# Sixteen attention items in float32: the product with v taken with the queries on partitions, a column of sums in v, and the division moved behind the product

## The chip, the cores and the metric

The kernel runs on one core of one Trainium2 chip. The metric is the device time of one launch in microseconds, the median of several runs. Five engines work side by side on it: TensorE (PE, its weight loads are listed as PEld), VectorE (DVE), ScalarE (ACT), GpSimd (POOL) and SyncE (SP), which here issues every transfer between memory and the on-chip buffers.

## What is computed

Attention with a window of 128 keys, then two feed-forward layers over the 2304 resulting tokens. Batch 4, heads 8, sequence 576, head size 64; d_model 512, d_ff 2048.

```python
scores = scale * np.matmul(q, k.transpose(0, 1, 3, 2))
scores = np.where(mask, scores + bias[None], -1000000000.0)
scores = scores - np.max(scores, axis=-1, keepdims=True)
attn = np.exp(scores)
attn = attn / (np.sum(attn, axis=-1, keepdims=True) + 1e-09)
attn_out = np.matmul(attn, v)
x = attn_out.transpose(0, 2, 1, 3).reshape(B * S, H * D)
h = x @ w_in;  g = np.maximum(h, 0.0) + alpha * np.minimum(h, 0.0);  x = g @ w_out
h = x @ w_in2; g = h * (1.0 / (1.0 + np.exp(-1.702 * h)));  out = g @ w_out2
```

The weights arrive as 64-bit floats and are decoded on the chip.

## The kernel before, in words

**Attention.** The work is cut into 64 items `(b, u, h)`: a batch, one of two pieces of the sequence (u = 0: queries 0 to 255; u = 1: the other 320) and a head. Items 0 to 15 (b = 0 and 1 of u = 0; `n < FP`) multiply in plain float32, which PE runs as two passes for every matmul; their rows in the trace count both. All later items split each operand into two parts of a faster type and take other branches. The steps of an item: `a_qk` (scores `s`, line 343), `a_bias` (DVE adds the position bias and takes the row minimum, 363), `a_exp` (ACT, 379, which also sums each row), `a_recip` (DVE, 387 and 388), `a_norm` (the weights `tt` times the reciprocal: one chunk of 128 keys on DVE, 399, one of 256 on ACT, 397), `a_trans` (PE transposes `tt` into `pt`, 412), `a_pt_hi` (ACT copies `pt` to the on-chip buffer, 419), `a_av` (PE multiplies with v, 433), `a_x3` (ACT rounds the result `x` into `xh`, 480, and DVE puts the rest into `xl`, 107).

For items 0 to 15 two heads share one result: `vz` holds v in one half of its columns and zeros in the other, so an even head fills partitions 0 to 63 of `x` and the odd head partitions 64 to 127. So `a_x3` works once for a pair of items. The tiles `s`, `pt` and `x` come from one pool of four banks (`ps_a`).

**First layer.** Blocks k of 256 tokens; block k of u = 0 needs the eight items of batch k. For each of 16 slices f of d_ff: `m1_h` (12 products into `h`, line 494, reading `xh`, `xl` and the weights `wh`, `wl`), an activation (ACT 509, DVE 519, ACT 523 and DVE 107 into `gh`, `gl`), and `m1_o`, two slices later (12 products into `o`, 545). Block 0 needs all of items 0 to 7, block 1 all of items 8 to 15.

**Weights.** The first layer has 32 chunks of 512 KB. A chunk is loaded into one of four `ws` buffers (131), scaled by ACT (147, 148), joined by DVE (152 `sign`, 157 `shift`, 162 `add`), rounded by ACT into `wh` (102) and the rest put into `wl` by DVE (107). The load of chunk i + 4 waits for the `add` of chunk i.

**Order.** The program is written as a loop over items 0 to 9 (lines 734 to 765) with two decode steps an item, then as steps (k, f) with an item every two steps (781 to 846). A scheduler with a timeline of its own puts the instructions of each engine in a fixed order from that; each engine runs its own list in order and waits where an operand is missing.

Of the kernel before, what the change touches and what calls it, by code (L numbers as in the profile page):

```python
# [11 lines left out]
F32 = mybir.dt.float32  # L12
# [3 lines left out]
AF = mybir.ActivationFunctionType  # L16
ALU = mybir.AluOpType
PSUM = bass.MemoryType.PSUM

B, H, S, D = 4, 8, 576, 64  # L20
NT, DM, DFF = 2304, 512, 2048
P = 128
# [12 lines left out]
         chunks=((256, 128, 128, 256), (384, 128, 256, 256), (512, 64, 384, 192))),  # L35
# [12 lines left out]
FP = 2 * H  # L48
# [17 lines left out]
def tile_window_attention__then__two_mlps(  # L66
# [13 lines left out]
    nc = tc.nc  # L80
# [10 lines left out]
    ident = const.tile([P, P], F32, name="ident")  # L91
# [30 lines left out]
    chunks = [(0, f, part) for f in range(NF) for part in range(2)]  # L122
# [134 lines left out]
    ps_a = at.enter_context(tc.tile_pool(name="ps_a", bufs=4, space=PSUM))  # L257
# [3 lines left out]
    sts = [ap_.tile([P, 16], F32, name=f"st{i}") for i in range(2)]  # L261
# [3 lines left out]

    af = ExitStack()
    apf = af.enter_context(tc.tile_pool(name="attf", bufs=1))
    vzs = [apf.tile([P, 2, P], F32, name=f"vz{i}") for i in range(2)]
    pts = [apf.tile([P, 384], F32, name=f"pt{i}") for i in range(2)]
    relht = apf.tile([P, H, 2 * P], BF16, name="relht")  # L270

# [13 lines left out]
    st = {}  # L285

    def raw_of(n):
        return (raws + rawfs)[n % 4] if n < H else raws[n % 2]
# [34 lines left out]
    @stage  # L323
    def a_split_v(n, b, u, h, U):
        nv = (2, 4)[u]
        vr = raw_of(n)[:, UCOLS[u] - nv * D : UCOLS[u]].rearrange("p (j d) -> p j d", d=D)
        if n < FP:
            d0 = (h % 2) * D
            nc.gpsimd.tensor_copy(vzs[n % 2][:, :, d0 : d0 + D], vr)
            return  # L330
        vp = ar["v", n % 2]
        nc.scalar.copy(vp[:, :nv, :D], vr)
        sub("pool", vp[:, :nv, D:], vr, vp[:, :nv, :D])
# [40 lines left out]
    @stage  # L374
    def a_exp(n, b, u, h, U):
        tt, s = tts[n % 2], sts[n % 2]
        for i, (c0, rows, kk, keys) in enumerate(U["chunks"]):
            t = tt[:rows, i * 256 : i * 256 + keys]
            nc.scalar.activation(
                t, t, AF.Exp, bias=s[:rows, i : i + 1], scale=-1.0, accum_out=s[:rows, 4 + i : 5 + i]  # L380
            )

    @stage
    def a_recip(n, b, u, h, U):
        s = sts[n % 2]
        m = len(U["chunks"])
        nc.vector.tensor_scalar(s[:, 8 : 8 + m], s[:, 4 : 4 + m], 1e-9, None, op0=ALU.add)
        nc.vector.reciprocal(s[:, 12 : 12 + m], s[:, 8 : 8 + m])  # L388

    @stage  # L390
    def a_norm(n, b, u, h, U, eng):
        tt, s = tts[n % 2], sts[n % 2]
        for i, (c0, rows, kk, keys) in enumerate(U["chunks"]):
            t = tt[:rows, i * 256 : i * 256 + keys]
            r = s[:rows, 12 + i : 13 + i]
            if eng == "act" or (eng == "mix" and i):
                nc.scalar.mul(t, t, r)
            else:
                nc.vector.tensor_scalar(t, t, r, None, op0=ALU.mult)
# [27 lines left out]
    @stage  # L427
    def a_av(n, b, u, h, U):
        if n < FP:
            x = st["x", n] = st["x", n - 1] if h % 2 else ps_a.tile([P, 512], F32, tag="a", name="x")  # L430
            pt, vz = pts[n % 2], vzs[n % 2]
            for j in range(2):
                nc.tensor.matmul(  # L433
                    x[:, j * P : 256], vz[:, j, :], pt[:, j * 256 : 256 + j * P],
                    start=(h % 2 == 0 and j == 0), stop=(h % 2 == 1 and j == 1), skip_group_check=True,
                )
            return
        vp = ar["v", n % 2]
        x = ps_a.tile([P, 512], F32, tag="a", name="x")
        js = (0, 1) if u == 0 else (2, 1, 3, 4)  # L440
        for i, j in enumerate(js):
            col, nq, oc = PTCOL[u][j]
            v = vp[:, j - U["k0"] // P, :]
            for k, p in enumerate((ar["pth"], ar["ptl"])):
                nc.tensor.matmul(  # L445
                    x[:, oc : oc + nq], v, p[:, col : col + nq],
                    start=(i == 0 and k == 0), stop=(i == len(js) - 1 and k == 1),
                    skip_group_check=True,
                )
        st["x", n] = x  # L450
# [17 lines left out]
    @stage  # L468
    def a_x3(n, b, u, h, U):
        if h % 2 == 0:  # L470
            return
        nq, c, xp = U["nq"], h // 2, xps
        if n < FP:
            xp = st["x", n]
        t = u * B * UNITS[0]["nq"] + b * nq
        done = 0
        while done < nq:
            r = (t + done) % RING
            w = min(nq - done, RING - r)
            nc.scalar.copy(xh[:, c, r : r + w], xp[:, done : done + w])  # L480
            sub("dve", xl[:, c, r : r + w], xp[:, done : done + w], xh[:, c, r : r + w])
            done += w
# [222 lines left out]


    for t in vzs:
        nc.gpsimd.memset(t, 0.0)
    for t in sts:
        nc.gpsimd.memset(t, 1.0)  # L710
    def w_first(n):
# [54 lines left out]
    n = H + 2  # L766
# [14 lines left out]
    for s, (k, f) in enumerate(steps):  # L781
        n = H + 2 + s // 2
# [181 lines left out]
```

## Time and profile before

| | us |
|---|---|
| median of 3 runs | 968.03 (967.75 to 969.53) |
| the profiled execution | 967.92 |
| its span, first to last instruction | 966.1 |
| PE busy | 939.6 (97%) |
| DVE busy | 721.6 (75%) |
| ACT busy | 536.4 (56%) |
| POOL busy | 89.8 (9%) |

The page gives busy time for the whole span. The kernel has a first stage of some 60 us, in which weights are decoded and items 0 to 9 are worked on side by side, and a long rest in which PE hardly pauses, so the shares of the whole say little of the first stage. For it the views by stretch of time and the rows of each engine in order of time are read.

### The profile page before, as it was taken

The page shows a single profiled execution, that of the slowest core. Times are in us where ns is not written, and L with a number is a line of the kernel's source. Part 1 is how long each engine was busy: PE and PEld are TensorE (multiplying, and loading weights), DVE is VectorE, ACT ScalarE, POOL GpSimd, SP SyncE. Part 2 cuts the span into 40 slices and gives each one's busy share as a digit, 9 for nine tenths or more (in the row PEclk, how much of TensorE's full clock was granted, in tenths as well). Part 3 has the DMA queues.
Part 4 walks back from the last instruction along what each step waited for, and adds up shares of the span by engine and source line. Part 5 has one row for each costly group of instructions (what it writes and reads, how often), then busy time and mean ns, then how long its engine had stood idle before and what let it go on. Part 6 is the DMA issues. An engine that isn't in the chain of part 4 may idle for free.

```text
span 966.1 us, 17886 instructions
## 1 busy us (share of the span) xinstructions
PE 939.6 (97%) x6536; PEld 871.2 (90%) x6536; DVE 721.6 (75%) x1789; ACT 536.4 (56%) x1343; POOL 89.8 (9%) x127
## 2 busy tenths in 40 slices
PE   5899999999999999999999999999999999999997
PEld 3579889999999999999988888888898889999997
DVE  6998967767888888887666864697233798878876
ACT  6987766666767667676534443564232644333433
POOL 1000021122222222222000000000000000000000
PEclk9999999999999999999999999999999999999999
DMA  8654521222222223212022335566432333443323
GB/s 266 187 185 148 184 79 56 78 72 66 89 67 88 67 66 89 67 66 89 1 69 81 124 112 182 186 219 200 155 113 88 140 140 114 142 142 113 132 85 109
DMA packets 43895, 112.44 MB, mean 116 GB/s; under 512 B 5024, under 2 KB 15008, under 8 KB 43808
## 3 DMA queue, kind: packets, MB, share of 16 engines
q1 hardware_dynamic: 43808, 111.31, 35.3%
q8 instruction: 51, 0.84, 0.3%
q14 instruction: 36, 0.29, 0.1%
HBM read 82.98 MB, written 28.31 MB: 115 GB/s over the span
## 4 chain that ended last, share of the span: by engine, by line
PE 92%; DMA 3%; ACT 2%; DVE 1%; issue 1%; SPq 0%; DVEq 0%; ACTq 0%
PE h L494 21%; PE h L592 20%; PE p L659 17%; PE o L545 17%; PE p L545 5%; PE x L445 3%; PE pt L412 3%; DMA ws<-in_w_out_dram 2%; PE s L352 1%; PE s L353 1%; PE s L343 1%; PE x L433 1%; ACT ws L148 1%; DMA ws<-in_w_in_dram 0%; ACT oh L102 0%
## 5 line engine op out<-in xcount | busy, mean ns | idle before, releaser
L494 PE MATMUL h<-xh,wh 128*128 128x256 f32 (+1 forms) x512 | 153.7, 302 | 1.0 <-ACT xh L480 0.7
L494 PE MATMUL h<-xh,wl 128*128 128x256 f32 (+1 forms) x512 | 153.6, 300 | 0.0
L494 PE MATMUL h<-xl,wh 128*128 128x256 f32 (+1 forms) x512 | 153.5, 300 | 0.1
L659 PE MATMUL p<-wh,oh 128*128 128x256 f32 x504 | 136.2, 284 | 1.0 <-ACT oh L102 0.6
L659 PE MATMUL p<-wl,oh 128*128 128x256 f32 x504 | 136.1, 283 | 0.0
L545 PE MATMUL o<-gh,wl 128*128 128x256 f32 x448 | 127.5, 286 | 0.0
L545 PE MATMUL o<-gh,wh 128*128 128x256 f32 x448 | 125.4, 286 | 0.0
L545 PE MATMUL o<-gl,wh 128*128 128x256 f32 x448 | 125.2, 281 | 0.0
L659 PE MATMUL p<-wh,ol 128*128 128x256 f32 x504 | 119.2, 284 | 1.0 <-DVE ol L107 1.0
L592 PE MATMUL h<-x2h,wh 128*128 128x512 f32 (+1 forms) x320 | 117.8, 368 | 0.0
L592 PE MATMUL h<-x2l,wh 128*128 128x512 f32 (+1 forms) x320 | 117.7, 368 | 0.0
L592 PE MATMUL h<-x2h,wl 128*128 128x512 f32 (+1 forms) x320 | 117.7, 368 | 0.0
L606 DVE TENSOR_TENSOR g<-h,sg 128x512 f32<-128x512 f32 (+1 forms) x80 | 51.0, 637 | 79.6 <-ACT sg L602 79.5
L602 ACT ACTIVATE sg<-h 128x512 f32<-128x512 f32 (+1 forms) x80 | 44.5, 556 | 107.2 <-PE h L592 106.9
L494 PEld LDWEIGHTS h<-xh,wh 128*128 128x128 f32 x512 | 97.9, 192 | 6.7 <-ACT xh L480 1.9
L494 PEld LDWEIGHTS h<-xl,wh 128*128 128x128 f32 x512 | 98.5, 192 | 5.0 <-DVE st L388 1.3
L494 PEld LDWEIGHTS h<-xh,wl 128*128 128x128 f32 x512 | 98.3, 192 | 2.9
L659 PEld LDWEIGHTS p<-wh,oh 128*128 128x128 f32 x504 | 96.4, 192 | 2.1 <-ACT oh L102 2.0
L659 PEld LDWEIGHTS p<-wl,oh 128*128 128x128 f32 x504 | 96.7, 192 | 0.1
L519 DVE SCALAR_TENSOR_TENSOR g<-n,beta,h 128x256 f32<-128x256 f32 x112 | 53.2, 476 | 46.6 <-ACT n L509 46.4
L659 PEld LDWEIGHTS p<-wh,ol 128*128 128x128 f32 x504 | 86.3, 192 | 1.7 <-DVE ol L107 1.6
L509 ACT ACTIVATE n<-h 128x256 f32<-128x256 f32 x112 | 42.8, 384 | 79.9 <-PE h L494 79.5
(107 smaller groups left out, 2270.7 us busy)
## 6 DMA issues: line engine op xcount, KB each, us to landing
ws<-in_w_in_dram SPq DMA_DIRECT2D x32, 512.0 KB, 3.6
ws<-in_w_out_dram SPq DMA_DIRECT2D x32, 512.0 KB, 3.9
raw<-in_u_dram SPq DMA_DIRECT2D x32, 512.0 KB, 3.4
g2d<-g SPq DMA_DIRECT2D x32, 512.0 KB, 3.4
gr<-g2d SPq DMA_DIRECT2D x32, 512.0 KB, 3.2
raw<-in_u_dram SPq DMA_DIRECT2D x16, 320.0 KB, 2.8
wd<-x2d SPq DMA_DIRECT2D x36, 128.0 KB, 3.0
out_dram<-ob SPq DMA_DIRECT2D x16, 256.0 KB, 3.9
```

Of the source, the lines that this page charges most:

```text
L148: pin(nc.scalar.mul(lo, lo.bitcast(U32), 2.0**-29))
L343: nc.tensor.matmul(o[:, :keys], raw[:, c0 : c0 + rows], raw[:, 256 + kk : 256 + kk + keys], start=True, stop=True)
L412: nc.tensor.transpose(banks[bank][:, dst : dst + P], src, ident)
L445: nc.tensor.matmul(x[:, oc : oc + nq], v, p[:, col : col + nq], start=(i == 0 and k == 0), stop=(i == len(js) - 1 and k == 1), skip_group_ ...
L494: nc.tensor.matmul(ph, w[:, 0, c * P : (c + 1) * P], x[:, c, r : r + n], start=(c == 0 and i == 0), stop=(c == NC - 1 and i == 2),)
L509: nc.scalar.activation(n, ph, AF.Relu, scale=-1.0)
L519: nc.vector.scalar_tensor_tensor(g, n, beta[:, f : f + 1], ph, op0=ALU.mult, op1=ALU.add)
L545: nc.tensor.matmul(o, w[:, 1, c * P : (c + 1) * P], g, start=(f == 0 and (k == KM or c % 2 == 0) and i == 0), stop=(f == NF - 1 and i == 2 ...
L592: nc.tensor.matmul(ph[:, :n], w[:, f % 2, c * P : (c + 1) * P], x[:, c, :n], start=(c == 0 and i == 0), stop=(c == NC - 1 and i == 2),)
L602: nc.scalar.activation(sg[:, :n], ph[:, :n], AF.Sigmoid, scale=1.702)
L606: nc.vector.tensor_tensor(g[:, f % 2, :n], ph[:, :n], sg[:, :n], op=ALU.mult)
L659: nc.tensor.matmul(o[:, m, :], g[:, a, m * P : (m + 1) * P], w, start=(p == 0 and m == 0 and i == 0), stop=(p == NF // 2 - 1 and i == 2), ...
```

## The change

For items 0 to 15 the transposed weights `pt` become the stationary operand and v the moving one, so the result `xq` has the queries on partitions. `vz` has 65 columns a key block: 64 of v and one of ones, so the last column of `xq` is the sum of the (not yet divided) weights. There are three matmuls an item, of 65 columns each, in place of one of 256 and one of 128. `a_exp` no longer sums, `a_recip` and `a_norm` do nothing for these items. After the odd item of a pair DVE adds 1e-9 to the four sums of the pair, takes the reciprocals and multiplies `xq` by them into the buffer tile `xq` (lines 445, 446, 448 of the changed kernel). `a_x3` first transposes that back with two PE transposes a pair into a new tile `x` (line 488), and goes on as before.

```diff
--- before.py
+++ after.py
@@ -265,7 +265,8 @@
 
     af = ExitStack()
     apf = af.enter_context(tc.tile_pool(name="attf", bufs=1))
-    vzs = [apf.tile([P, 2, P], F32, name=f"vz{i}") for i in range(2)]
+    vzs = [apf.tile([P, 2, D + 1], F32, name=f"vz{i}") for i in range(2)]
+    xq = apf.tile([P, 2, 2, D], F32, name="xq")
     pts = [apf.tile([P, 384], F32, name=f"pt{i}") for i in range(2)]
     relht = apf.tile([P, H, 2 * P], BF16, name="relht")
 
@@ -325,8 +326,7 @@
         nv = (2, 4)[u]
         vr = raw_of(n)[:, UCOLS[u] - nv * D : UCOLS[u]].rearrange("p (j d) -> p j d", d=D)
         if n < FP:
-            d0 = (h % 2) * D
-            nc.gpsimd.tensor_copy(vzs[n % 2][:, :, d0 : d0 + D], vr)
+            nc.gpsimd.tensor_copy(vzs[n % 2][:, :, :D], vr)
             return
         vp = ar["v", n % 2]
         nc.scalar.copy(vp[:, :nv, :D], vr)
@@ -376,6 +376,9 @@
         tt, s = tts[n % 2], sts[n % 2]
         for i, (c0, rows, kk, keys) in enumerate(U["chunks"]):
             t = tt[:rows, i * 256 : i * 256 + keys]
+            if n < FP:
+                nc.scalar.activation(t, t, AF.Exp, bias=s[:rows, i : i + 1], scale=-1.0)
+                continue
             nc.scalar.activation(
                 t, t, AF.Exp, bias=s[:rows, i : i + 1], scale=-1.0, accum_out=s[:rows, 4 + i : 5 + i]
             )
@@ -384,13 +387,15 @@
     def a_recip(n, b, u, h, U):
         s = sts[n % 2]
         m = len(U["chunks"])
+        if n < FP:
+            return
         nc.vector.tensor_scalar(s[:, 8 : 8 + m], s[:, 4 : 4 + m], 1e-9, None, op0=ALU.add)
         nc.vector.reciprocal(s[:, 12 : 12 + m], s[:, 8 : 8 + m])
 
     @stage
     def a_norm(n, b, u, h, U, eng):
         tt, s = tts[n % 2], sts[n % 2]
-        for i, (c0, rows, kk, keys) in enumerate(U["chunks"]):
+        for i, (c0, rows, kk, keys) in enumerate(U["chunks"] if n >= FP else ()):
             t = tt[:rows, i * 256 : i * 256 + keys]
             r = s[:rows, 12 + i : 13 + i]
             if eng == "act" or (eng == "mix" and i):
@@ -427,13 +432,20 @@
     @stage
     def a_av(n, b, u, h, U):
         if n < FP:
-            x = st["x", n] = st["x", n - 1] if h % 2 else ps_a.tile([P, 512], F32, tag="a", name="x")
+            x = st["xq", n] = st["xq", n - 1] if h % 2 else ps_a.tile([P, 2, 2, D + 1], F32, tag="a", name="xq")
             pt, vz = pts[n % 2], vzs[n % 2]
-            for j in range(2):
+            for c, j, col in ((0, 0, 0), (1, 0, 128), (1, 1, 256)):
                 nc.tensor.matmul(
-                    x[:, j * P : 256], vz[:, j, :], pt[:, j * 256 : 256 + j * P],
-                    start=(h % 2 == 0 and j == 0), stop=(h % 2 == 1 and j == 1), skip_group_check=True,
+                    x[:, c, h % 2, :], pt[:, col : col + P], vz[:, j, :],
+                    start=(c == j == h % 2 == 0), stop=(c == j), skip_group_check=True,
                 )
+            if h % 2:
+                s = sts[n % 2]
+                r = s[:, 8:12].rearrange("p (c h) -> p c h", c=2)
+                nc.vector.tensor_scalar(r, x[:, :, :, D], 1e-9, None, op0=ALU.add)
+                nc.vector.reciprocal(s[:, 12:16], s[:, 8:12])
+                r = s[:, 12:16].rearrange("p (c h) -> p c h", c=2)
+                nc.vector.tensor_tensor(xq, x[:, :, :, :D], r.unsqueeze(3).to_broadcast([P, 2, 2, D]), op=ALU.mult)
             return
         vp = ar["v", n % 2]
         x = ps_a.tile([P, 512], F32, tag="a", name="x")
@@ -471,7 +483,9 @@
             return
         nq, c, xp = U["nq"], h // 2, xps
         if n < FP:
-            xp = st["x", n]
+            xp = ps_a.tile([P, 512], F32, tag="a", name="x")
+            for i in range(2):
+                nc.tensor.transpose(xp[:, i * P : (i + 1) * P], xq[:, i, :, :], ident)
         t = u * B * UNITS[0]["nq"] + b * nq
         done = 0
         while done < nq:
@@ -705,7 +719,7 @@
 
 
     for t in vzs:
-        nc.gpsimd.memset(t, 0.0)
+        nc.gpsimd.memset(t, 1.0)
     for t in sts:
         nc.gpsimd.memset(t, 1.0)
     def w_first(n):
```

The diff moves no call, yet the scheduler makes other lists of it. Three places of them follow. The digits behind a name tell its buffer and its tile apart; a number after `wl`, as in `wl7`, is the slice f.

DVE, kernel before, in the first stage around the row that completes the input of block 0 (`xl` of items 6 and 7):

```order
L107 TENSOR_TENSOR wl7_534<-wd_506,wh7_533 128x512
L162 ISA wd_519<-ws_463,wd_519 128x1024
L152 TENSOR_SCALAR ws_474<-ws_474 128x512
L387 TENSOR_SCALAR st1_149<-st1_149 128x2
L157 SCALAR_TENSOR_TENSOR wd_552<-wd_552,ws_474 128x512
L107 TENSOR_TENSOR xl_132<-x_522,xh_131 128x256
```

and the changed kernel at the same `xl`:

```order
L107 TENSOR_TENSOR wl8_572<-wd_557,wh8_571 128x512
L448 TENSOR_TENSOR xq_160<-xq_519,st1_149 128x256
L107 TENSOR_TENSOR wl9_661<-wd_586,wh9_660 128x512
L162 ISA wd_602<-ws_544,wd_602 128x1024
L152 TENSOR_SCALAR ws_555<-ws_555 128x512
L152 TENSOR_SCALAR ws_584<-ws_584 128x512
L157 SCALAR_TENSOR_TENSOR wd_651<-wd_651,ws_555 128x512
L107 TENSOR_TENSOR xl_132<-x_589,xh_131 128x256
```

The weights of slice 9 are being split where those of slice 7 were: counted from the top of DVE's list down to this row, 17 `sign`, 17 `shift`, 16 `add` and 15 `wl` rows have become 22, 21, 20 and 19.

PE, changed kernel, in the middle of block 0 (the transposes back of items 10 and 11):

```order
L559 MATMUL o1_755<-gh_902,wl5_445 128x256
L559 MATMUL o0_754<-gh_958,wh6_485 128x256
L559 MATMUL o1_755<-gh_958,wh6_485 128x256
L488 MATMUL x_913<-ident_72,xq_160 128x128 x2
L417 MATMUL pt_945<-ident_72,tt0_146 128x128 x3
L343 MATMUL s_949<-raw1_145 128x128
```

The row of line 488 is new. It reads what DVE writes with line 448, and everything below it on PE stands behind it.

PE, kernel before, where block 0 ends and block 1 begins (`h_1481` and `h_1533` are the first slices of block 1):

```order
L545 MATMUL o1_758<-gl_1467,wh15_1310 128x256
L545 MATMUL o1_758<-gh_1463,wl15_1311 128x256
L412 MATMUL pt_1281<-ident_72,tt1_147 128x128
L352 MATMUL s_1285<-kh_153,q_152 128x192
L353 MATMUL s_1285<-kl_154,q_152 128x192
L352 MATMUL s_1285<-kh_153,q_152 128x256
L353 MATMUL s_1285<-kl_154,q_152 128x256
L412 MATMUL pt_1281<-ident_72,tt1_147 128x128 x2
L433 MATMUL x_1229<-pt1_161,vz1_159 128x256
L433 MATMUL x_1229<-pt1_161,vz1_159 128x128
L494 MATMUL h_1481<-xh_131,wh0_226 128x256
```

and the changed kernel at the same place:

```order
L508 MATMUL h_1435<-xh_131,wl15_1305 128x256
L488 MATMUL x_1364<-ident_72,xq_160 128x128 x2
L417 MATMUL pt_1396<-ident_72,tt0_146 128x128 x3
L352 MATMUL s_1400<-kh_153,q_152 128x192
L353 MATMUL s_1400<-kl_154,q_152 128x192
L352 MATMUL s_1400<-kh_153,q_152 128x256
L353 MATMUL s_1400<-kl_154,q_152 128x256
L559 MATMUL o0_754<-gh_1360,wh13_1080 128x256
```

Before, the last float32 product with v stood behind the last `o` product of block 0 and right ahead of block 1. Now the last product with v stands 47 rows ahead of block 1, whose first product follows the 12 `o` products of slice 13 that begin with the last row here; the 24 `o` products of slices 14 and 15 come after that.

## Rows read from the trace of the kernel before

**Rows 1.** The page: busy us, share of span, instructions
```profile
PE 939.6 (97%) x6536; PEld 871.2 (90%) x6536; DVE 721.6 (75%) x1789; ACT 536.4 (56%) x1343; POOL 89.8 (9%) x127
```
**Rows 2.** Stretches: length, busy PE, PEld, DVE, ACT, POOL, PEclk, DMA share, GB/s
```profile
20.00:60.00 40.00, 34.98 (x102) 23.93 (x102) 36.11 (x104) 35.57 (x87) 3.53 (x8) 1.00 0.66 204
67.40:112.00 44.60, 44.58 (x353) 42.22 (x352) 40.14 (x100) 34.22 (x83) 1.11 (x3) 1.00 0.49 156
112.00:129.00 17.00, 14.59 (x94) 12.93 (x95) 11.43 (x40) 12.42 (x38) 3.38 (x7) 0.90 0.52 169
```
**Rows 3.** Timeline of DVE: start us, busy us, line, operation [idle before it]
```profile
21.83 0.43 DVE L152 TENSOR_SCALAR ws<-ws 128x512 int32<-128x512 int32 x1 [0.89 <-ACT wd L147]
...
59.24 0.42 DVE L107 TENSOR_TENSOR xl<-x,xh 128x256 fp32r<-128x256 f32 x1
...
95.30 0.42 DVE L107 TENSOR_TENSOR xl<-x,xh 128x256 fp32r<-128x256 f32 x1
```
**Rows 4.** Timeline of DVE, a stretch without a wait
```profile
49.38 0.40 DVE L107 TENSOR_TENSOR xl<-x,xh 128x256 fp32r<-128x256 f32 x1
49.70 0.68 DVE L107 TENSOR_TENSOR wl<-wd,wh 128x512 fp32r<-128x512 f32 x1
50.30 0.69 DVE L162 CUSTOM_DVE_ANT_0 wd<-ws,wd 128x1024 uint16<-128x1024 uint16 x1
50.90 0.32 DVE L399 TENSOR_SCALAR tt<-tt,st 128x128 f32<-128x128 f32 x1
51.14 0.15 DVE L387 TENSOR_SCALAR st<-st 128x2 f32<-128x2 f32 x1
51.21 0.42 DVE L152 TENSOR_SCALAR ws<-ws 128x512 int32<-128x512 int32 x1
51.54 0.16 DVE L388 RECIPROCAL st<-st 128x2 f32<-128x2 f32 x1
51.66 0.69 DVE L157 SCALAR_TENSOR_TENSOR wd<-wd,ws 128x512 int32<-128x512 int32 x1
52.27 0.42 DVE L152 TENSOR_SCALAR ws<-ws 128x512 int32<-128x512 int32 x1
```
**Rows 5.** Timeline of PE, first stage, products that follow one another
```profile
66.52 0.41 PE L494 MATMUL h<-xh,wl 128*128 128x256 f32 x1
66.74 0.41 PE L494 MATMUL h<-xh,wh 128*128 128x256 f32 x1
```
**Rows 6.** Timeline of PE in block 0 behind the first stage
```profile
76.23 0.49 PE L412 MATMUL pt<-ident,tt 128*128 128x128 f32 x3
76.65 0.92 PE L343 MATMUL s<-raw 64*128 64x128 f32 x4
77.50 0.39 PE L494 MATMUL h<-xh,wh 128*128 128x256 f32 x1
...
79.86 0.81 PE L433 MATMUL x<-pt,vz 128*128 128x256 f32 x4
...
80.64 0.28 PE L545 MATMUL o<-gl,wh 128*128 128x256 f32 x1
80.76 0.28 PE L545 MATMUL o<-gh,wl 128*128 128x256 f32 x1
```
**Rows 7.** Timeline of PE in a later item, products of 64 columns
```profile
242.00 0.22 PE L445 MATMUL x<-pth,vp 128*128 128x64 f32 x1
242.05 0.28 PE L445 MATMUL x<-ptl,vp 128*128 128x64 f32 x1
242.16 0.37 PE L545 MATMUL o<-gh,wl 128*128 128x256 f32 x1
```
**Rows 8.** Timeline of PE where block 0 gives way to block 1
```profile
112.64 0.89 PE L433 MATMUL x<-pt,vz 128*128 128x256 f32 x4 [0.66 <-ACT pt L419]
...
123.88 0.92 PE L433 MATMUL x<-pt,vz 128*128 128x256 f32 x4 [0.88 <-ACT pt L419]
125.51 0.74 PE L494 MATMUL h<-xh,wh 128*128 128x256 f32 x2 [0.71 <-ACT xh L480]
```

## The prediction

> **What bounds the kernel now.** PE is busy for 97% of the span [rows 1], so the end comes when PE has done its list; a change of 16 items out of 64 pays or costs through the time that PE loses, and through the work that it is given. The views by stretch say where it loses. From 20 to 60 us DVE is busy 36.1 of 40 us and ACT 35.6 [rows 2]: both are nearly full with decoding and items 0 to 9. PE shows 35.0 busy there, but at half pace: products of 256 columns follow one another 0.21 to 0.22 us apart [rows 5], which is 256 columns at 1.2 GHz, against 0.12 later [rows 6]. From 67.4 to 112 us PE does not pause (44.58 of 44.60), and DVE is full at 40.1 [rows 2]. From 112 to 129 us PE loses again: three waits of 0.66, 0.88 and 0.71 us for the last two pairs of items [rows 8], and a granted clock of 0.90 over these 17 us [rows 2], which is another 0.10 x 17 = 1.7 us. Behind 129 us the lists of the two kernels are the same and PE has no gap to fill. So the question is when PE gets the input of block 0 (`xl` of items 6 and 7, now at 59.24 us [rows 3]), what it must do and wait for from there, and whether the 3.9 us around 112 to 129 us come back.
>
> The sum is made against the profiled execution, 967.92 us, 0.1 below the median. A measurement of this kernel can tell about 0.2%, 1.9 us, from no change.
>
> **Part 1, the first stage: +7.2 us.** DVE runs its list in order. Two things happen to that list. Each pair of items loses two times `1e-9`, reciprocal and norm (0.07, 0.12 and 0.24 us from one row's start to the next [rows 4], 0.86 a pair) and gets one add over four sums, one reciprocal and one multiplication of 256 columns from PSUM. For the add I take 0.1 us, near the 0.07 of line 387; for the multiplication 0.33, as `xl`, which also reads 256 columns from PSUM, takes from 49.38 to 49.70 [rows 4]: 0.55 a pair, so 0.3 us a pair are saved. But the scheduler has put more decoding ahead of the `xl` of items 6 and 7. From the `sign` of the sixth chunk (at 21.83 us [rows 3], held by the transfer through ACT, and so left where it is) down to that `xl`, DVE's list had 12 `sign`, 12 `shift`, 12 `add` and 12 `wl` rows; now 17, 16, 15 and 15. The prices are 0.33, 0.61, 0.60 and 0.60 us [rows 4]: 5 x 0.33 + 4 x 0.61 + 3 x 0.60 + 3 x 0.60 = 7.7 us more. In the same rows 7, 6 and 6 of the three small ones go, 0.49 + 0.72 + 1.44 = 2.7, four pairs of new ones come, 2.2, so 7.2 us remain and the row moves from 59.2 to 66.4 us. From below: DVE idles 3.9 of the 40 us from 20 to 60 [rows 2], partly for ACT, which is relieved of 16 norms and 32 reads of row sums; if all that goes, 3.3 remain. From above: the stretch keeps its idle share of 10% on the added work too, 7.9. I take the value without either, since the transfers of the chunks are drawn closer together as well. What hides nothing here: while DVE decodes ahead, PE has only the items, and its list stands still until `xl` is there.
>
> **Part 2, what PE does from there: -2.0 us.** Seven products with v remain (items 9 to 15). One takes now 80.64 - 79.86 - 0.12 = 0.66 us [rows 6]. The new one is six passes of 65 columns. Its columns alone, at the rate of the old ones (0.66 us for 768 columns in four passes), take 390 x 0.86 ns = 0.33 us. In a later item, passes of 64 columns with a weight load each start 0.05 and 0.11 us apart [rows 7]; I take the mean less a little, 0.07, so 0.42 us, with 0.33 and 6 x 0.11 = 0.66 as ends. That saves 7 x 0.24 = 1.7. The transposes back cost two passes of 128 columns a pair, 0.24 us by the 0.12 of a product of as many column cycles, 1.0 for four pairs. The transposes of item 9 and the scores of item 10 (77.50 - 76.23 = 1.27 us [rows 6]) now stand above the row at which PE waits and run under that wait: -1.3. Sum -2.0; from -2.6 to -0.3. The products of the items up to 8 lie under DVE and count nothing; POOL's copies and fills are smaller and POOL is idle nine tenths of the time [rows 2].
>
> The Trainium skill, TensorE: Matmul & The Clock Gate, section LDWEIGHTS (loading the stationary operand), says that a weight load lasts as many cycles at 1.2 GHz as it has columns, which is 107 ns for 128. This change trades long moving operands for short ones behind full loads, so the rule speaks against it. The two starts 0.05 us apart [rows 7] do not agree with it as a bound on the pace. By the rule the product costs 0.64 us and Part 2 comes to about -0.5, an estimate from that page.
>
> **Part 3, the new wait: +1.9 us.** PE's two transposes back (line 488) wait for DVE's multiplication (448), and on PE everything behind them waits too: the next product with v, the scores that DVE's next bias needs, and `h` and `o`. For the pair 10 and 11 DVE's list has 67 rows from `xl` of items 6 and 7 to that multiplication. In the kernel before the 82 rows between the `xl` of these two pairs took 95.30 - 59.24 = 36.1 us [rows 3], 0.44 a row, so DVE gets there after 29.5 us. PE has until then 162 products of 0.12 (19.4), two sets of transposes and scores (2.5), three products with v (1.3), one set of transposes back (0.2), some 3.5 us lost at half pace, as now between 59.7 and 67.4, and under 1 us of seams: 27.6. The difference is 1.9. It is nothing if DVE's rows, relieved of waits, go at 0.41; it is some 4 if the pairs 8/9 and 12/13 wait as well. Behind that row decoding ends and DVE has room.
>
> **Part 4, the end of block 0: -3.9 us.** In the list before, the last product with v is the last thing ahead of block 1, all `o` products of block 0 being done: hence the waits of rows 8. In the new list 47 rows lie between, and 24 `o` products are left over. The three waits (2.25) and the lost clock (1.7) should go. From above: none of it goes, 0.
>
> Sum: 7.2 - 2.0 + 1.9 - 3.9 = +3.2, so 967.92 + 3.2 = **971.1 us**. With the ends of each term it could lie between about 963 and 980; they will not all fall on one side. SP's list loads chunks earlier among the items' transfers and moves nothing that PE waits for, as far as its order shows. One more tile a pair in the four banks of `ps_a` makes waits only on the same DVE rows.
>
> **The rivals.**
>
> *Faster: DVE was slowed by its neighbours, not by its list.* ACT loses 16 norms and 32 sum reads and is as full as DVE in the first stage [rows 2]; DVE's waits for ACT, like the 0.89 us of rows 3, go with them. Then Part 1 is 3.3, Part 3 is 0: 3.3 - 2.0 - 3.9 = -2.6, 965.3 us. It decides where `xl` of items 6 and 7 starts: below about 63 us the kernel is faster. Against it: DVE idles only a tenth of that time, and a longer list cannot be undone by fewer waits. Chance 0.27.
>
> *Slower by more: the end of block 0 keeps its loss.* If the four rows of line 488 each find DVE late, the waits move and the clock falls again; Part 4 gives 0, and the sum is 7.1, 975.0 us. For it: DVE is full up to 112 us [rows 2]. Against it: decoding ends earlier in the new list. Chance 0.15.
>
> *The product gains nothing.* If the weight loads set the pace, by 6 x 0.11 us or by the rule of the page above, Part 2 is about -0.4 and the time 972.7 us. Chance 0.10.
>
> **How the numbers follow.** My forecast, 971.1, has 0.48; its own range is 968 to 974, of which about 0.20 lies within 1.9 us of no change and 0.28 above. Of the faster rival 0.22 lies below 966.1 and 0.05 inside; of the third 0.02 inside. Together: faster 0.22, same 0.27, slower 0.51. The range reaches from the faster rival's 965.3 to the slower one's 975.0, with a little added at both: 965.0 to 975.5.
>
> **What would show it.** In the new profile DVE's `xl` for items 6 and 7 should start near 66 us, and PE should be less busy from 20 to 66 than now. The products should run unbroken at 0.12 us from some 73 us on, with a wait of one to two us ahead of a transpose of line 488 between 85 and 97 us, and none ahead of block 1, where the granted clock should stay 1.00. Passes of line 438 should start about 0.07 us apart at full pace. I am wrong if that `xl` starts near 60 us or earlier, if PE still waits at the start of block 1, or if the passes start 0.11 us apart.

## The result, and the profile after

| | before | changed |
|---|---|---|
| median of 4 runs, us | 967.89 (967.00 to 969.53) | 975.46 (973.73 to 975.84) |
| ratio, 95% interval | | 1.0073 (1.0055 to 1.0091) |
| the profiled execution, us | 967.92 | 973.73 |
| its span, us | 966.1 | 971.9 |

The changed kernel is slower by 0.73%. The profiled execution is the fastest of its four and lies 5.8 us above that of before; what follows explains these 5.8 us.

The page of the changed kernel (busy us, share of span, instructions), beside [rows 1]:

```profile
PE 937.0 (96%) x6584; PEld 874.2 (90%) x6584; DVE 717.7 (74%) x1765; ACT 528.2 (54%) x1295; POOL 88.9 (9%) x127
```

PE, DVE, ACT and POOL are all less busy (only PE's weight loads, PEld, a little more), and the kernel takes longer. Stretches of the changed kernel, columns as in [rows 2]:

```profile
20.00:60.00 40.00, 29.13 (x110) 22.85 (x110) 36.63 (x96) 32.87 (x66) 2.98 (x6) 1.00 0.68 209
...
112.00:129.00 17.00, 17.00 (x144) 16.50 (x142) 9.30 (x33) 9.05 (x29) 1.89 (x5) 1.00 0.11 30
```

In the first stage PE is busy 29.1 us instead of 35.0. Around the start of block 1 it does not pause and its granted clock is 1.00: the waits of [rows 8] are gone. So the loss is made earlier, ahead of block 0. What PE waits for there (changed kernel, waits of PE from 20 to 80 us: us in total, times, longest):

```profile
PE x L488 <- DVE xq L448: 14.2, 4, 4.4
PE h L508 <- DVE g L533: 1.2, 1, 1.2
PE xq L438 <- ACT pt L424: 0.4, 1, 0.4
```

Four times, once a pair of items, PE stands in front of the transposes back, 14.2 us in all. The last of them on PE, changed kernel:

```profile
59.99 1.38 PE L438 MATMUL xq<-vz,pt 128*128 128x65 f32 x6
65.10 0.66 PE L488 MATMUL x<-ident,xq 128*128 128x128 f32 x2 [3.73 <-DVE xq L448]
65.55 1.38 PE L438 MATMUL xq<-vz,pt 128*128 128x65 f32 x6
66.73 0.84 PE L417 MATMUL pt<-ident,tt 128*128 128x128 f32 x3
67.51 1.65 PE L343 MATMUL s<-raw 64*128 64x128 f32 x4
```

and what DVE does in these 5 us, and the `xl` that completes the input of block 0:

```profile
61.44 0.15 DVE L445 TENSOR_SCALAR st<-xq 128x4 f32<-128x4 f32 x1
61.97 0.43 DVE L152 TENSOR_SCALAR ws<-ws 128x512 int32<-128x512 int32 x1 [0.38 <-ACT wd L147]
62.32 0.68 DVE L162 CUSTOM_DVE_ANT_0 wd<-ws,wd 128x1024 uint16<-128x1024 uint16 x1
62.92 0.17 DVE L446 RECIPROCAL st<-st 128x4 f32<-128x4 f32 x1
63.01 0.66 DVE L157 SCALAR_TENSOR_TENSOR wd<-wd,ws 128x512 int32<-128x512 int32 x1
63.93 0.69 DVE L107 TENSOR_TENSOR wl<-wd,wh 128x512 fp32r<-128x512 f32 x1 [0.26 <-ACT wh L102]
64.54 0.41 DVE L448 TENSOR_TENSOR xq<-xq,st 128x256 f32<-128x256 f32 x1
...
68.27 0.42 DVE L107 TENSOR_TENSOR xl<-x,xh 128x256 fp32r<-128x256 f32 x1
```

The division itself is some 0.7 us of work, but its three rows have decode rows between them, and from the first to the end of the last 3.5 us pass. Behind the waiting row on PE stand the product of item 8, the transposes of item 9's weights and the scores of item 10. `xl` of items 6 and 7 starts at 68.27 us instead of 59.24 [rows 3].

From there on PE hardly loses. It reaches full pace here (changed kernel, timeline of PE; [rows 5, 6] for the two paces), 8.5 us later than the kernel before, whose PE came to it at 67.4:

```profile
75.64 0.41 PE L508 MATMUL h<-xh,wl 128*128 128x256 f32 x1
75.85 0.36 PE L508 MATMUL h<-xh,wh 128*128 128x256 f32 x1
76.06 0.28 PE L508 MATMUL h<-xl,wh 128*128 128x256 f32 x1
```

and a later transposition back and a product, at full pace and without a wait, against [rows 6]:

```profile
78.43 0.38 PE L488 MATMUL x<-ident,xq 128*128 128x128 f32 x2
78.65 0.49 PE L417 MATMUL pt<-ident,tt 128*128 128x128 f32 x3
...
82.50 0.79 PE L438 MATMUL xq<-vz,pt 128*128 128x65 f32 x6
83.10 0.36 PE L508 MATMUL h<-xh,wh 128*128 128x256 f32 x1
83.30 0.28 PE L508 MATMUL h<-xl,wh 128*128 128x256 f32 x1
```

Behind the old product, [rows 6] leave out the first row (kernel before):

```profile
80.43 0.36 PE L545 MATMUL o<-gh,wh 128*128 128x256 f32 x1
```

So the second row behind the product starts 0.78 us after it in the kernel before (79.86 to 80.64) and 0.80 us after it in the changed one (82.50 to 83.30): the new product is no shorter than the old. The rows of one product are shown as one. Asked for short stretches within it, the trace gives the second and the third of the six passes:

```profile
82.57 0.50 PE L438 MATMUL xq<-vz,pt 128*128 128x65 f32 x3
82.68 0.50 PE L438 MATMUL xq<-vz,pt 128*128 128x65 f32 x3
```

The first pass is followed after 0.07 us, the others after 0.11.

The account of the 5.8 us, by when PE has done the same work in both traces: +9.0 at `xl` of items 6 and 7; +8.5 at full pace; +5.2 behind block 1 (the 469th product of `h`, at 203.3 us before and 208.5 changed); +5.8 at the end. The last 0.6 us come behind 680 us, far from the change.

### The profile page after: what moved, and what is told of

Same layout as the page of the kernel before. It is cut to its first block, busy times and chain, and to the rows that moved or that the text cites. A ratio compares the mean times of both kernels' runs of the same rounds, so it can differ in the third digit from the quotient of the medians.

```text
span 971.9 us, 17890 instructions
## 1 busy us (share of the span) xinstructions
PE 937.0 (96%) x6584; PEld 874.2 (90%) x6584; DVE 717.7 (74%) x1765; ACT 528.2 (54%) x1295; POOL 88.9 (9%) x127
## 3 DMA queue, kind: packets, MB, share of 16 engines
q1 hardware_dynamic: 43808, 111.31, 35.6%
## 5 line engine op out<-in xcount | busy, mean ns | idle before, releaser
L533 DVE SCALAR_TENSOR_TENSOR g<-n,beta,h 128x256 f32<-128x256 f32 x112 | 53.2, 476 | 55.3 <-ACT n L523 54.9
```

What stands on the lines that cost most here:

```text
L533: nc.vector.scalar_tensor_tensor(g, n, beta[:, f : f + 1], ph, op0=ALU.mult, op1=ALU.add)
```

## The experiments

The forecast's theory, **A**, was DVE's list: the scheduler puts more decoding ahead of that `xl`. The rival, **B** (later **H**), is the chain: PE waits for DVE's division at the head of its own list, and the items behind it come late. Each run was timed against the kernel before on its chip, but for the last, which is one execution with its profile. The first loads land up to 2.7 us apart from one execution to another, so starts are compared from the third row of scores (line 343), a row that waits for them: 12.76 us before, 12.85 changed. The table has, for the profiled execution of each, the decode rows ahead of `xl` of items 6 and 7, PE's waits in front of the transposes back of the first four pairs, DVE's busy time from 20 to 60 us, that `xl` counted from the third scores, and the ratio to the kernel before on the same chip.

| kernel | sign/shift/add/wl | PE's waits, us | DVE busy of 40 | `xl`, us | ratio (95%) |
|---|---|---|---|---|---|
| before | 17/17/16/15 | none there | 36.1 | 46.5 | |
| before_again | the same | none there | 37.2 | 45.2 | |
| changed | 22/21/20/19 | 14.2 | 36.6 | 55.4 | 1.0073 (1.0055 to 1.0091) |
| after_again | the same | 14.1 | 35.6 | 54.5 | 1.0094 (1.0078 to 1.0109) |
| first8 | 22/20/20/19 | 15.2 | 36.0 | 55.2 | 1.0083 (1.0068 to 1.0098) |
| last8 | 17/17/16/16 | none there | 35.5 | 47.6 | 1.0015 (0.9997 to 1.0032) |
| wide | 22/21/20/19 | 12.9 | 35.1 | 54.9 | 1.0079 (1.0050 to 1.0107) |
| held | 14/14/14/13 | 11.0 | 29.6 | 49.3 | 1.0132 (1.0107 to 1.0158) |
| same_ahead | 17/16/16/15 | 14.0 | 30.5 | 53.5 | 1.0085 (1.0070 to 1.0100) |
| two | 20/19/19/18 | 8.4 | 37.0 | 50.0 | 1.0049 (1.0036 to 1.0061) |
| late | 17/16/15/14 | 1.9 | 32.8 | 48.6 | 1.0007 (0.9993 to 1.0021) |
| late_two | 15/15/14/14 | 0.2 | 32.5 | 44.3 | 1.0005 (0.9994 to 1.0016) |
| late_ahead | 21/20/19/18 | 2.7 | 31.5 | 59.9 | 1.0133 (1.0119 to 1.0147) |
| before_late | 20/20/20/18 | none there | 36.9 | 54.6 | 1.0154 (1.0129 to 1.0179) |

**Where in the program: last8 and first8.** The change with `new(n)` in place of `n < FP`:

```diff
+    new = lambda n: H <= n < FP
...
-            if n < FP:
+            if new(n):
```

for `last8`, and `n < H` for `first8`; both keep two sets of `vz` tiles, zeros and ones.

> The change for items 8 to 15 alone; items 0 to 7 as in the kernel before. DVE's decode rows ahead of `xl` of items 6 and 7 are then 17, 17, 16, 16, nearly those of the kernel before. Theory A (the loss is made in the first stage, by the list that the scheduler makes of items 0 to 7): `xl` at 59 to 60 us, and what the change gives behind it, 2.2 to 2.8 us of the waits and the lost clock of the end of block 0 less the transposes back, remains as a gain: 964 to 966.5 us. Rival D (the waits of the end of block 0 went only because block 0 began 9 us later): the waits stay, 967.5 to 970.

Measured: `xl` at 60.4 on the clock of the kernel before (47.6 + 12.8), as A expected, but the time is that of before, not 2 to 3 us less. The waits ahead of block 1 did not stay either, as D would have it: only 0.2 to 0.3 us each are left. What was gained there was lost at the head of block 0, on PE:

```profile
PE h L522 <- DVE g L547: 2.0, 1, 2.0
```

> The change for items 0 to 7 alone; items 8 to 15 as in the kernel before. Ahead of `xl` of items 6 and 7: 22, 20, 20, 19 decode rows, as in the changed kernel. All theories: `xl` at 67 to 69 us from the common start. If the waits and the lost clock at the end of block 0 (3.9 us in the kernel before) go because block 0 starts later and not because of the new steps of items 8 to 15, they are gone here too, and the time is that of the changed kernel or up to 1 us less, 972 to 976. If the new steps of items 8 to 15 take them away, they are back: 976 to 979.

Measured: `xl` at 67.9, 974.83 us. The waits ahead of block 1 are gone here too, with the old steps of items 8 to 15. So items 0 to 7 alone make the whole loss; the last decode row starts at 109 us as in the changed kernel (107.7), instead of 117, and that is enough to clear the end of block 0.

**Less decoding ahead: held and same_ahead.** In both, the `sign` rows are held behind the DVE rows that the program has ahead of them; in `same_ahead` only in part, so that the counts are those of the kernel before.

```diff
     def w_sign(i):
...
-        pin(nc.vector.tensor_scalar(hi, hi, -0x80000000, None, op0=ALU.bitwise_and))
+        ins = nc.vector.tensor_scalar(hi, hi, -0x80000000, None, op0=ALU.bitwise_and)
+        (tc.keep_in_program_order if held else pin)(ins)
```

> The changed kernel with one thing added: in the first stage each chunk's `sign` row keeps its place behind the DVE row that the program has ahead of it, so that the scheduler cannot move decoding up. Ahead of `xl` of items 6 and 7 stand now 14 sign, 14 shift, 14 add and 13 wl rows, where the changed kernel has 22, 21, 20, 19 and the kernel before 17, 17, 16, 15. Theory A (the list: the first stage is longer because DVE decodes further ahead): that `xl` starts at 60 us or earlier instead of 68.3, and since the waits of the end of block 0 stay away the time falls to 962 to 968 us. Theory B (the chain: PE waits for DVE's division, 2.4 to 4.4 us in front of each of the four transposes back of the first stage, and the items come late whatever DVE decodes): DVE idles in the room it gets, `xl` starts at 65 us or later, and the time is 972 to 977. Rival C (decoding put off is missed later): `xl` is early, but PE waits for `wl` in block 0, 970 to 976.

Measured: 979.2 us, slower than the changed kernel. `xl` came 6 us earlier for 14.1 us of rows taken away, to 62.0 on the clock of the kernel before, later than A has it, and the decoding put off was missed, as rival C has it but by more. Waits of PE from 100 to 140 us:

```profile
PE h L509 <- ACT wh L102: 4.8, 2, 2.7
PE pt L418 <- ACT tt L381: 1.2, 1, 1.2
```

> The changed kernel with the `sign` rows held behind the program's earlier DVE rows in iterations 0 to 6 and, for the second decode step of an iteration, everywhere: ahead of `xl` of items 6 and 7 stand 17 sign, 16 shift, 16 add and 15 wl rows, as in the kernel before (17, 17, 16, 15), and the lists behind keep close to it (28, 27, 27, 25 at the next but one `xl` against 27, 26, 26, 24). Against the changed kernel 5 x 0.33 + 5 x 0.61 + 4 x 0.60 + 4 x 0.60 = 9.5 us of DVE work stand behind that `xl` instead of ahead of it. Times of rows are counted from a common start, the third row of scores (line 343, at 12.8 us in both kernels), since the first loads land up to 2 us apart from run to run. Theory A (list alone): `xl` at 58.8 us, and 964 to 966 us. Theory B (the new chain holds the items whatever DVE decodes): `xl` at 65 us or later. Theory M (list and chain: the run in which decoding was held back furthest had it at 62.0 with DVE idle for 8 us, so the chain has a floor there): `xl` at 61.5 to 63 us, DVE with 6 to 8 us idle in 20 to 60 us, and 967 to 970 us.

Measured: 974.71 us, no better than the changed kernel. This is the run that fells A, the list by itself: 9.5 us of DVE work went from ahead of `xl`, and it moved by 1 to 2 us, to 66.2 on the clock of the kernel before. The room stayed empty, and PE's waits stayed (`same_ahead`: DVE's stretch and `xl`, PE's waits from 20 to 80 us, DVE's from 20 to 68; its lines are one higher here: 489 and 449 are 488 and 448, 418 is 417 and 364 is 363):

```profile
20.00:60.00 40.00, 31.43 (x117) 24.22 (x115) 30.52 (x82) 28.29 (x57) 2.93 (x6) 1.00 0.55 162
```

```profile
66.94 0.42 DVE L107 TENSOR_TENSOR xl<-x,xh 128x256 fp32r<-128x256 f32 x1
```

```profile
PE x L489 <- DVE xq L449: 14.0, 4, 5.5
```

```profile
DVE wl L107 <- ACT wh L102: 6.2, 9, 1.5
DVE tt L364 <- PE pt L418: 3.5, 5, 1.0
```

The last row shows a circle. PE waits for DVE's division; the transposes of an item's weights stand behind it on PE; and DVE's bias of the item after next, which writes the same buffer `tt`, waits for those transposes. It is a part of the room only, and `late` below has 4.0 us of it as well. DVE's waits for ACT, 6.2 us, are longer; the changed kernel has 4.1 us of them in the same stretch (3.2 for `wd`, 0.9 for `wh`), so they can have taken back about 2 of the 9.5 us. And the decode rows still stand inside the division: for pair 6/7 its addition starts at 61.15 us and its multiplication at 64.83, 3.7 us apart against 3.1 in the changed kernel. The count ahead of `xl` fell, the chain stayed.

**PE taken out of the wait: late, late_two, two.** `late` keeps all of the change and only calls `a_x3` of the first three pairs one item later; the transposes back of items 0 to 7 are held behind the PE rows that the program has ahead of them:

```diff
-        a_x3(n - 2)
+        a_x3(n - 3 if n < H + 1 else n - 2)
```

> The changed kernel with the two transposes back of the pairs 0/1, 2/3 and 4/5 placed one item later in the program, behind the transposes of the next item's weights; pair 6/7 as it was. PE no longer stands at them with the next items behind it. The scheduler by itself then puts 17 sign, 16 shift, 15 add and 14 wl rows ahead of `xl` of items 6 and 7 (22, 21, 20, 19 in the changed kernel): 5 x (0.33 + 0.61 + 0.60 + 0.60) = 10.7 us of DVE work less. Theory A (list alone): `xl` at 57.6 us. Theory M (list and chain): the three waits of 2.4, 4.4 and 3.7 us of line 488 shrink below 1.5 us each and `xl` comes at 58 to 60, earlier than with the decoding of the kernel before and the chain left as it is (61.5 to 63). Theory B': the chain is only moved to pair 6/7, whose wait stays at 3 to 4 us, and `xl` is at 63 or later. Time: 962 to 967 us by A and M, if the end of block 0 stays free of waits; 968 to 972 by B' or if the decoding that is put off is missed before block 1.

Measured: 967.58 us, the time of the kernel before, so all of the loss is recovered, with nearly as many decode rows ahead as `same_ahead` has (one `add` and one `wl` fewer). `xl` is at 61.4 on the clock of the kernel before, between M and B'. The first stage is not back to what it was: the first product of `o` starts at 72.45 us, against 68.42 before and 77.36 in the changed kernel (0.9 us of the 4.0 by the third row of scores, which starts later), and it is the end of block 0, without waits here too, that pays the rest back. The three moved rows wait no more; pair 6/7 waits 1.9 us. The third of them and the waits of PE from 20 to 80 us in `late`:

```profile
51.50 0.90 PE L417 MATMUL pt<-ident,tt 128*128 128x128 f32 x3
52.20 0.63 PE L488 MATMUL x<-ident,xq 128*128 128x128 f32 x2
```

```profile
PE xq L438 <- ACT pt L424: 2.2, 5, 1.1
PE x L488 <- DVE xq L448: 1.9, 1, 1.9
PE h L510 <- DVE g L535: 1.7, 1, 1.7
PE xq L438 <- issue: 1.6, 1, 1.6
```

> As the kernel with the transposes back one item later, and DVE takes the reciprocals straight from the four sums, so that two rows stand between the product and the transposes back instead of three; the addition of 1e-9 is left out. Ahead of `xl` of items 6 and 7: 15 sign, 15 shift, 14 add, 14 wl rows. Theory M: a shorter chain brings that `xl` another 1 to 2 us forward, to 57 to 59 us, time 961 to 966 us. Theory C (DVE's decoding is as much a bound as the items: what is put off is missed before block 1): PE waits for `wl` or `wh` between 105 and 130 us, as in the run in which decoding was held back furthest, and the time is no better than with three rows.

Measured: `xl` at 57.0, as expected and earlier than in the kernel before, but 967.40 us, no better than with three rows. Of C's waits there are two for ACT of 0.3 and 0.4 us at 118 us, too small to be it. A wait of 2.0 us for DVE's `g` (line 533) stands at the head of block 0, behind decode rows; what took the rest was not tried.

> The changed kernel with the transposes back where the change has them, but two DVE rows in front of them instead of three: the reciprocals are taken straight from the four sums, the addition of 1e-9 is left out. Ahead of `xl` of items 6 and 7: 20 sign, 19 shift, 19 add, 18 wl rows. By theory H each pair's wait in front of line 488 loses the row and the decode row that stands between it and the next, some 0.7 to 1.2 us: waits of 1.5 to 3.5 us instead of 2.4 to 4.4, `xl` 2 to 4 us earlier than 68.2, at 64 to 66, and 969 to 972 us. By theory A the list gives 2 x 0.33 + 2 x 0.61 + 0.60 + 0.60 = 3.1 us, `xl` at 65. The run does not tell H from A; it prices one row of the chain.

Measured: 970.59 us, `xl` at 62.7, earlier than both theories said. One row less in the chain took 5.8 us from PE's waits (14.2 to 8.4) and about 5 from the start of `xl`, more than the 3.1 us of decode rows that left the list with it. The run takes from both, so it does not part them.

**More decoding ahead: before_late and late_ahead.** Extra decode steps are called ahead of `xl`, which is held behind them:

```diff
+        for _ in range(6 if n == H + 1 else 0):
+            for x in ("split", "sign", "shift", "add"):
+                w(x)
```

for `before_late`; in `late_ahead` one step each in iterations 6, 8 and 9.

> The kernel before, with nothing of the change, but six decode steps moved ahead of `xl` of items 6 and 7 (and that row held behind them): 20 sign, 20 shift, 20 add, 18 wl rows ahead of it instead of 17, 17, 16, 15, which by rows 4 is 3 x 0.33 + 3 x 0.61 + 4 x 0.60 + 3 x 0.60 = 7.0 us of DVE work. Theory A (the list alone costs it): `xl` starts near 66 us and PE's full pace some 7 us later than in the kernel before. If the waits at the end of block 0 are there because of the old order of steps, 974 to 976 us; if a later start of block 0 takes them away by itself, 970 to 972. Theory B (only the new chain of PE and DVE costs): within 1.5 us of the kernel before, 967 to 969.5.

Measured: 981.54 us, worse than any expectation. It doesn't price the list alone: `xl` is 8 us later than before for 7.0 us of rows, but the norms of items 8 and 9 were pushed back as well, and PE stood 10.4 us in three waits for them (waits of PE from 55 to 90 us):

```profile
PE pt L412 <- DVE tt L399: 10.4, 3, 5.0
```

> The kernel with the transposes back of the first three pairs one item later, and now with decoding put ahead again: three more decode steps in iterations 6, 8 and 9, and the `xl` rows of items 2 to 7 held behind them. Ahead of `xl` of items 6 and 7 stand 21 sign, 20 shift, 19 add and 18 wl rows instead of 17, 16, 15, 14: 4 x (0.33 + 0.61 + 0.60 + 0.60) = 8.6 us of DVE work more, nearly the changed kernel's list (22, 21, 20, 19) without its waits of PE in front of line 488. With it the two causes stand in all four combinations. Theory H (PE's wait in front of the transposes back holds up the items behind it; the decoding ahead only fills the room that this leaves): DVE has 7.2 us idle from 20 to 60 us in the kernel without the extra decoding, most of the 8.6 go there, `xl` at 61 to 64 us from the common start, time 967 to 970 us. Theory A2 (once the wait is gone the list counts in full): `xl` at 68 to 70 and 973 to 976 us.

Measured: 978.53 us, `xl` at 72.7 on the clock of the kernel before: later than even A2 allows, for 8.6 us of rows. DVE stayed as idle as without them (31.5 busy of 40), because the held rows wait for ACT and hold up all rows behind them. H's claim that the rows would go into the idle time fell. So decoding ahead of `xl` does cost where `xl` must wait for it; what its own price is, free of the hold, stays open. So does what the removal of the wait alone would give back: no run has the long list without the wait and without the hold.

**The product: wide.**

```diff
-    vzs = [apf.tile([P, 2, D + 1], F32, name=f"vz{i}") for i in range(2)]
+    vzs = [apf.tile([P, 2, P], F32, name=f"vz{i}") for i in range(2)]
```

and the result tile as wide.

> The changed kernel with 128 columns moved in each of the three products with v instead of 65 (63 more columns of ones, the result as wide); the same number of passes and weight loads, and the same decode rows ahead of `xl` of items 6 and 7 (22, 21, 20, 19). If the weight load of 128 columns sets the pace of a pass, the product stays at the 0.59 us that it takes at full pace in the changed kernel (82.50 to 83.10), and the time within 1 us of it. If the columns set it, or load and columns add up, a pass grows by up to 63 columns x 0.86 ns = 0.054 us, the product to 0.9 us, and the time by 6 to 7 products x 0.33 = 2.0 to 2.3 us.

Measured: 974.35 us, like the changed kernel, and the product as long as with 65 columns, 0.59 us (timeline of PE, `wide`):

```profile
92.01 0.83 PE L438 MATMUL xq<-vz,pt 128*128 128x128 f32 x6
92.60 0.37 PE L508 MATMUL h<-xh,wl 128*128 128x256 f32 x1
```

At full pace 128 columns take no longer than 65. So the columns do not set the pace there; that the load of 128 columns of weights does, which recurs with each pass, is the explanation left, and no run varied it.

**Both kernels again.**

> The changed kernel once more, unedited, on the chip of the other runs: its time beside theirs (972 to 977 us), and whether the places on which the reading rests come back in a second trace: `xl` of items 6 and 7 at 67 to 69 us from the common start, four waits of line 488 for DVE of 2 to 5 us each in the first stage and none later, the product at full pace in 0.58 to 0.60 us, no wait between 80 and 130 us.

Measured: 975.13 us; `xl`, the four waits (2.4, 4.6, 3.1 and 4.0 us; the first is put down to ACT) and the unbroken stretch came back.

> The kernel before once more, unedited, with a profile: whether the third row of scores can start up to 2 us later than 12.8 us in this kernel too (a landing of the first loads, no work of the kernel), as in the runs of the edited kernels; `xl` of items 6 and 7 at 59 to 60 us from that start; the waits ahead of block 1 again 2 to 2.5 us in all, with a granted clock below 0.95 from 112 to 129 us.

Measured: third scores at 12.37 us, 0.4 earlier, not later; in nine of the ten edited kernels and in `after_again` they stand at 13.5 to 15.1. Whether that is chance or belongs to the edits stays open; the ratios of whole runs contain it. `xl` came at 58.0 on the common clock, 1.3 us before the first trace's, and the waits ahead of block 1 were there again (waits of PE from 100 to 130 us):

```profile
PE x L433 <- ACT pt L419: 1.5, 2, 0.9
PE h L494 <- ACT xh L480: 0.7, 1, 0.7
PE h L494 <- DVE g L519: 0.5, 1, 0.5
```

The last thing expected did not come: the granted clock from 112 to 129 us is 1.00, not below 0.95, and the products at the start of block 1 are 0.12 us apart, where in the first trace they are 0.21 (`before_again`, stretch and timeline of PE):

```profile
112.00:129.00 17.00, 14.87 (x113) 13.60 (x114) 11.78 (x40) 13.02 (x42) 3.63 (x8) 1.00 0.47 152
```

```profile
124.61 0.28 PE L494 MATMUL h<-xh,wl 128*128 128x256 f32 x1
124.73 0.28 PE L494 MATMUL h<-xl,wh 128*128 128x256 f32 x1
```

So the waits ahead of block 1 belong to the kernel, but the lost clock does not come with every execution. The span here is 963.1 us, 3.0 less than in the first trace: about 2 us are gained by the start of block 1 and 1 us there.

No version beat the kernel before: `late_two` comes nearest, with an interval that holds 1.

## Why the prediction was right and wrong

The sign was right and the size too small: 3.2 us against 5.8 in the profiled execution, some 7.6 between the medians, and 9.4 when the changed kernel ran again (975.13 against 965.72). The measured 975.46 lies 0.04 us below the upper end of the range, 975.5. That end was taken from a rival that did not happen, so it is luck that the range holds. By its steps:

- **Part 1, the first stage: +7.2 forecast, +9.0 measured, and for the wrong reason.** The step that failed is the sentence that while DVE decodes ahead "PE has only the items, and its list stands still until `xl` is there". The new wait that Part 3 priced only for items 10 and 11 stands four times in the first stage, 14.2 us in all, and there too others wait behind it. `same_ahead` shows that the list alone was not the bound: with the old count of rows `xl` moved by 1 to 2 us, and the time stayed. `late` shows that the loss goes when the wait goes too: with nearly the same count as `same_ahead`, and PE out of three of the four waits, `xl` came 4.9 us earlier than there and the time fell to that of before. That the longer list is only what the scheduler put into the room that the chain leaves is argued, not shown: without the wait it put 17, 16, 15 and 14 rows there of its own, but `late_ahead`, with the long list and little of the wait, is slower than the changed kernel. That the sum of the list came within 1.8 us of the truth is no support for it.
- **Part 2, PE's own work: -2.0 forecast, about +0.4 measured.** From `xl` to full pace the changed kernel gains 0.6 us (+9.0 to +8.5): item 9's transposes and item 10's scores did run ahead of block 0, but what that saved went mostly into a new wait of 1.2 us for `g`. The four later transposes back cost 0.22 us a pair (78.43 to 78.65), close to the forecast 0.24, 0.9 in all. The product is the term that was mis-sized: by the prediction's own measure (second row behind it, less 0.12) it is 83.30 - 82.50 - 0.12 = 0.68 us, against 0.66 before and 0.42 forecast, so nothing is saved where 1.7 us were expected. I had taken 0.07 us a pass from [rows 7]; the passes start 0.11 us apart. Those rows are of a later item, whose operands are of another type than plain float32, so they were the wrong neighbours. The Trainium skill, TensorE: Matmul & The Clock Gate, section LDWEIGHTS (loading the stationary operand), would have the load of each pass at 0.107 us. At full pace the measured 0.11 agrees with that and not with my 0.07; at half pace the passes start 0.21 us apart, which does not agree with it.
- **Part 3, the wait at items 10 and 11: +1.9 forecast, 0 measured.** From 76 to 129 us PE waits nowhere for line 488. With `xl` late, the decoding is done early, and DVE is ahead of PE there.
- **Part 4, the end of block 0: -3.9 forecast, and in this pair of traces it came.** There is no wait and a granted clock of 1.00 from 112 to 129 us. From +8.5 to +5.2 are -3.3 us, with the 0.9 of the transposes back inside, so some 4.2 us came back; the three waits of [rows 8] are 2.25 of them, and the remainder, some 2 us, is put down to the clock. But the clock's share is a matter of the execution: the second trace of the kernel before has the waits and keeps 1.00. The reason given, the new order of steps, was enough but not needed: `last8` has the new steps with `xl` near its old place and is left with waits of 0.2 to 0.3 us; `first8` has the old steps of these items, starts block 0 late, and loses nothing there either.

The errors went both ways: Parts 1 and 2 were together some 4 us too low, Part 3 was 1.9 us too high. The rival with the same size, 975.0, was not what happened: the end of block 0 kept no loss. The rival that the product gains nothing was right in its mechanism, and alone too small. Of the signs named in the prediction, `xl` was late and block 1 free of waits, as forecast; the wait at 85 to 97 us was absent; and the passes were 0.11 us apart, which it had named as a sign of being wrong.

## What to carry over

Where a change puts a step of another engine between two steps of PE (here product, division on DVE, transposes back), price the wait wherever it occurs, also where PE is not the bound: ask what stands behind the waiting row in PE's list and whose input that is. The work need not be undone: called one item later, behind rows that are ready, the same steps left the kernel as fast as before (ratio 1.0007, 0.9993 to 1.0021). And rows that a scheduler has moved may fill a gap rather than make it; take them away in one run before you hold them for its cause. A price per pass is to be taken from rows of the same operand type, and two products are to be compared by rows of the same place behind them.

## What the hardware showed

- At full pace three plain float32 products of 65 columns (six passes) and three of 128 columns take the same 0.59 us to the next row, and their passes start 0.11 us apart. At half pace the 65 columns take 1.18 us (65.55 to 66.73 in the changed kernel), with passes 0.21 us apart: what sets the pace of a pass follows the clock.
- The profile's granted clock can miss the half pace. In the changed kernel it reads 1.00 throughout the first stage, though products of 256 columns start 0.21 us apart up to 75.85 us. In the second trace of the same kernel it reads 0.50, the 1.2 GHz level, where they do so (stretches of `after_again`, columns as in [rows 2], and its timeline of PE):

```profile
66.00:75.00 9.00, 7.46 (x30) 6.32 (x31) 8.52 (x22) 7.05 (x15) 1.13 (x2) 0.50 0.73 221
```

```profile
74.72 0.41 PE L508 MATMUL h<-xl,wh 128*128 128x256 f32 x1
74.94 0.41 PE L508 MATMUL h<-xh,wl 128*128 128x256 f32 x1
```

- The landing of the first loads moved the third row of scores between 12.37 and 15.11 us, as here in `after_again`:

```profile
15.07 1.22 PE L343 MATMUL s<-rawf 64*128 64x128 f32 x3 [5.42 <-DMA rawf<-in_u_dram]
```

  That is as much as some of the differences under study: parts of two traces are to be compared from a common row, not from the start of the span.

- The same three waits ahead of block 1 (0.66, 0.88 and 0.71 us) were followed by a granted clock of 0.50 from 126 to 128 us in one execution of the kernel before, and by 1.00 throughout in the other.
